# Attention feeding a two-layer network: products of a step before its ReLUs, wider rows for the first keys and values, other store rooms and queues

## The chip, the cores and the metric

The kernel runs on one core of a Trainium2 chip. The metric is the device time of one execution in microseconds. TensorE (PE) multiplies matrices into PSUM, VectorE (DVE) and ScalarE (ACT) work elementwise, GpSimd (POOL) helps, SyncE (SP) issues most transfers, and 16 DMA engines move the data.

## The reference

```python
# attention over 32 memories per head; batch 8, 8 heads, 576 tokens, 64 wide
a = exp(phi - max(phi, axis=2)); a = a / (sum(a, axis=2) + 1e-9)      # over tokens
k_m = einsum('bhsm,bhsd->bhmd', a, k); v_m = einsum('bhsm,bhsd->bhmd', a, v)
scores = q @ k_m.T / sqrt(64)
attn = softmax(scores)                                               # over the 32 memories
x = (attn @ v_m) as 4608 tokens x 512
h = maximum(x @ w_in, 0)                                             # 2048 wide
return (h * h) @ w_out                                               # 4608 x 512
```

## The kernel before, in words

The work has two stages, and its order on each engine is the order in which the program is written.

The **first layer** never builds x. For each batch, `exp_phi` takes the exponent of phi, `memories` multiplies it with keys and values into 32 memories per head (a column of ones beside the values, in rows of 130, sums the denominators), `make_u` multiplies the value memories with a quarter of w_in into `u`, and `attend` makes the attention weights `a` of one token tile. Both `u` and `a` are kept as a high and a low part. A batch has a wide tile (320 tokens) and a narrow one (256). One `step` makes 128 rows of h for both tiles: three products (high x high, low x high, high x low) for each of two groups of heads, so six products for a tile, into one half of the PSUM tile `h`, then a ReLU on ACT (L496) into a room `o`. PSUM has two such tiles (`ps_f`). Two steps fill a room `o`, and `spill` stores it to DRAM on SP's queue (L506); the room's name goes by the step's number within its batch, and there are two rooms.

There are 130 steps: 10 in an order written out by hand (`ORDER`, where S is a step and the letters are the next piece of a task), then 120 in the main loop, in which `plan` names for each task the half steps behind which its pieces are issued. The weights arrive as 64-bit words that `decode_in` and `decode_out` turn into floats. The loads of batch 1 are issued together by `loads_1`, those of later batches by `plan`: phi by `load_phi`, keys and values by `load_kv` (two transfers of 512-byte rows for each pair of row blocks), q by `load_q` into one of two rooms. `spin` issues products whose results nobody reads.

The **second layer** loads h back, squares it, and multiplies it with w_out by a scheme with seven products of half-size blocks in place of eight (`products`, L606). `rooms_m` holds its results before they are added and stored.

The pools `ffn` and `att` hold the rooms of the first layer; the pools `s` and `x` of the second layer take their place.

```python
            for j, (v, x, qd) in enumerate(todo):
                nc.tensor.matmul(
                    h[:, i, :T], u[:, v, qd, fs], a[x][:, qd], start=j == 0, stop=j == len(todo) - 1
                )
            nc.scalar.activation(r[:, f % 2, x0:x0 + T], h[:, i, :T], AF.Relu)
```

Of the kernel before, what the change touches and what calls it, by code (L numbers as in the profile page):

```python
# [1 line left out]

# [6 lines left out]
F32 = mybir.dt.float32  # L9
# [13 lines left out]
def attn_moe_kernel(ctx: ExitStack, tc: tile.TileContext, qT, kv, phi, w_in, w_out, outT):  # L23
# [4 lines left out]
    P = 128  # L28
# [40 lines left out]
    ident = const.tile([P, P], F32, name="ident")  # L69
    make_identity(nc, ident)  # L70
    warm = const.tile([P, 8], F32, name="warm")
    nc.gpsimd.memset(warm, 0.0)
    const.tile([P, 24], F32, name="gap_wo")
    wo = [None] * NP

# [8 lines left out]
    A_TILES = [(f"a_{n}{t}", t) for t in range(NT) for n in ("hi", "lo")]  # L84
    for n, t in A_TILES:
        ffn.tile([P, NQ * width(t)], F32, name=f"{n}_1")
    for i in range(2):
        ffn.tile([P, 2 * S], F32, name=f"o{i}")
    for n, t in A_TILES:
        keep.tile([P, NQ * width(t)], F32, name=f"{n}_0")  # L90
# [9 lines left out]
    e_sb = att.tile([P, FULL * NQ * P + P], F32, name="e_sb")  # L100
    e_full = e_sb[:, :FULL * NQ * P].rearrange("p (c x) -> p c x", c=FULL)
    e_rest = e_sb[:, FULL * NQ * P:]
    kv_full = [att.tile([P, FULL, 4, CW], F32, name=f"kv{qd}") for qd in range(NQ)]
    kv_rest = att.tile([P, 4, CW], F32, name="kv_rest")
    for t in kv_full:
        nc.gpsimd.memset(t[:, :, :, 2 * D:], 1.0)
    nc.gpsimd.memset(kv_rest[:, :, 2 * D:], 1.0)

    starting = [True]
    fine = [True]  # L110
# [67 lines left out]
    def load_kv(b, queues=None):  # L178

        queues = queues or 6 * [nc.sync]  # L180
        todo = [(qd, c) for c in range(0, FULL + 1, 2) for qd in range(NQ)]
        for (qd, c), queue in zip(todo, queues):
            if c < FULL:
                x = kv[b, qd, c * P:(c + 2) * P].rearrange("(c p) h x -> p c h x", p=P)
                for k in range(2):
                    queue.dma_start(out=kv_full[qd][:, c + k, :, :2 * D], in_=x[:, k])  # L186
            else:
                queue.dma_start(out=kv_rest[D * qd:D * (qd + 1), :, :2 * D], in_=kv[b, qd, FULL * P:])
            yield

    def memories(b):

        assert ("phi", b) in ready
        acc = pair()

        def add(qd, j, x, y, c):
            nc.tensor.matmul(  # L197
                acc[M * j:M * (j + 1), qd, :CW], x, y, start=(c == 0), stop=(c == FULL),
            )

        for c in range(FULL):
            for qd in range(NQ):
                for j in range(4):
                    at = qd * P + M * j
                    add(qd, j, e_full[:, c, at:at + M], kv_full[qd][:, c, j], c)
        for j in range(4):
            for qd in range(NQ):
                hs = slice(D * qd, D * (qd + 1))
                add(qd, j, e_rest[hs, M * j:M * (j + 1)], kv_rest[hs, j], FULL)
        if starting:  # L210
            spin(2)
        ready.add(("read", b))
        yield
        den = att.tile([P, NQ], F32, name="den")
        nc.vector.tensor_scalar_add(den, acc[:, :, 2 * D], EPS)
        nc.vector.reciprocal(den, den)
        kvn = att.tile([P, 2, NQ, 2, D], F32, name="kvn")
        for qd in range(NQ):
            x = acc[:, qd, :2 * D].rearrange("p (x d) -> p x d", x=2)[:, :, None, :].broadcast_to([P, 2, 2, D])
            if starting and qd == 0:  # L220
                nc.vector.tensor_scalar_mul(kvn[:, :, qd], x, den[:, qd:qd + 1])
            else:
                nc.scalar.activation(kvn[:, :, qd], x, AF.Copy, scale=den[:, qd:qd + 1])
        yield
        tp = pair()[:, 0]
        for i in range(2 * NQ):
            nc.tensor.transpose(
                tp[:, i * P:(i + 1) * P], kvn[:, i // NQ, i % NQ].rearrange("p a d -> p (a d)"), ident
            )
        if starting:  # L230
            spin(1, k=3)
        yield
        mem = mems[b] = keep.tile([P, 2, NPAIR, M], F32, name=f"mem{b % 2}")
        for half in range(2):
            copy = nc.vector.tensor_copy if starting and not half else nc.scalar.copy
            hs = slice(D * half, D * (half + 1))
            copy(mem[hs], tp[hs].rearrange("p (x r h m) -> p x r h m", x=2, r=NPAIR, h=2)[:, :, :, half])
        ready.add(("mem", b))
# [5 lines left out]

    def load_q(b, t):
        t0, t1 = tokens(t)
        x = q_at[b, t] = att.tile([P, NPAIR, t1 - t0], F32, name=f"q{t}")
        for i in range(2):
            nc.sync.dma_start(  # L249
                out=x[:, NQ * i:NQ * (i + 1)],  # L250
                in_=qT[b, NQ * i:NQ * (i + 1), :, t0:t1].rearrange("a p s -> p a s"),
            )
# [62 lines left out]
    def first_softmax(T, st, flat, at, mx, sm, sc):  # L315
# [10 lines left out]
        for i in range(NQ):  # L326
            nc.vector.tensor_reduce(out=mx[:, of[i]], in_=x[i], axis=AX.X, op=ALU.max)
            if i == 0:
                spin(3)
        for i in range(NQ):  # L330
            nc.vector.tensor_tensor(out=x[i], in0=x[i], in1=by_block(mx, i), op=ALU.subtract)
            nc.scalar.activation(x[i], x[i], AF.Exp, scale=SCALE)
        spin(1, mx[:, :1].broadcast_to([P, P]))
        yield
        for i in range(NQ):
            nc.vector.tensor_reduce(out=sm[:, of[i]], in_=x[i], axis=AX.X, op=ALU.add)
        nc.vector.tensor_scalar_add(sm, sm, EPS)
        nc.vector.reciprocal(sm, sm)
        spin(3, sm[:, :1].broadcast_to([P, P]))
        yield  # L340
        for i in range(NQ):
            nc.vector.tensor_tensor(out=x[i], in0=x[i], in1=by_block(sm, i), op=ALU.mult)
# [2 lines left out]
        yield  # L345
        a_hi, a_lo = new_a(0, 0)
        for i in range(NQ):
            spin(2, x[i][:, :P // M], k=2)
            nc.scalar.copy(a_hi[:, i], at[:, i])
        for i in range(NQ):  # L350
            nc.vector.tensor_tensor(out=a_lo[:, i], in0=at[:, i], in1=a_hi[:, i].bitcast(F32), op=ALU.subtract)
# [120 lines left out]
    steps += [(b, both, f) for b in range(2, B) for f in range(NFT)]  # L472
    BASE = {b: 2 * steps.index((b, both, 0)) for b in range(2, B)}
    open_pair = {}

    def step(b, ts, f):

        n = f * P // FC
        fs = slice(f * P % FC, f * P % FC + P)
        u = u_at[b, n][0]  # L480
        h = ps_f.tile([P, 2, 512], F32, name="f")
        assert ("u", b, f * P) in ready, (b, f)
        if f % 2 == 0:
            open_pair[ts] = ffn.tile([P, 2, sum(width(t) for t in ts)], F32, name=f"o{f // 2 % 2}")
        r = open_pair[ts]
        x0 = 0
        for i, t in enumerate(ts):
            assert ("a", b, t) in ready, (b, t, f)
            a = a_at[b, t]
            T = width(t)  # L490
            todo = [(v, x, qd) for qd in range(NQ) for v, x in ((0, 0), (1, 0), (0, 1))]
            for j, (v, x, qd) in enumerate(todo):
                nc.tensor.matmul(  # L493
                    h[:, i, :T], u[:, v, qd, fs], a[x][:, qd], start=j == 0, stop=j == len(todo) - 1
                )
            nc.scalar.activation(r[:, f % 2, x0:x0 + T], h[:, i, :T], AF.Relu)  # L496
            x0 += T
        u_at[b, n][2] -= len(ts)
        if not u_at[b, n][2]:
            u_free.append(u_at[b, n][1])  # L500

    def spill(b, ts, f):
        if f % 2:
            s0 = b * S + tokens(ts[0])[0]
            r = open_pair.pop(ts)
            nc.sync.dma_start(out=r_f32[f // 2][:, :, s0:s0 + r.shape[-1]], in_=r)  # L506


    def second_layer():
# [99 lines left out]
                    )  # L609

        def rooms_m():
            m = [sp.tile([P, 2, 2 * HALF], F32, name=n) for n in ("m01", "m23")]
            m.append(xp.tile([P, 2, 2 * HALF], F32, name="m45", bufs=1))
            m6 = xp.tile([P, 2 * HALF], F32, name="m6", bufs=1)
            xp.tile([P, 8], F32, name="gap_m", bufs=1)
            return [x[:, i] for x in m for i in range(2)] + [m6]
# [108 lines left out]
    def all_of(tasks):  # L725
        for _ in tasks:
            pass

    load_phi(0, nc.scalar)
    all_of(load_kv(0, (nc.scalar, nc.sync, nc.sync, nc.scalar, nc.scalar, nc.sync)))  # L730
    fetch_in(0, NQ)
    load_q(0, 0)
    load_q(0, 1)
    for n in (1, 2, 3):
        fetch_in(n)
    nc.scalar.activation(warm[:1, :1], warm[:1, :1], AF.Exp)
    spin(3)
    spin(1, k=2)

    def loads_1():  # L740
        load_phi(1)
        all_of(load_kv(1))
        load_q(1, 0)
        load_q(1, 1)
        for n in range(4, 8):
            fetch_in(n)

    first = {
        "e": lambda: exp_phi(0),
# [12 lines left out]
        "b1": lambda: attend(1, 1),  # L762
    }
    for n in range(8):
        first[f"d{n}"] = lambda n=n: decode_in(n, nc.gpsimd if n < 1 else None)

    ORDER = """
        e*6 m*4 L a d0 a d0*3 a d0 d1 a u0 a u0*2
        b S S b*4 d1*4 b*3 d2 b u1 b u1*2 S S S S
        d2*3 e1*2 d2 e1 u2 e1 u2*2 S S  # L770
        d3 e1*2 d3*3 e1 d3 m1*2 u3*3 S S m1*2
        d4 a1*4 d4*2 a1*3 d4*2 a1*2 d5 b1 a1 v0*3 b1*3 d5*2 b1*3 d5*2 b1*3 v1*3
    """
    tasks = {}
    ended = set()
    for x in ORDER.split():
        x, _, k = x.partition("*")
        for _ in range(int(k or 1)):
            if x == "S":
                s = run_step()  # L780
                spill(*s)
            elif x == "L":
                loads_1()
            else:
                if x not in tasks:
                    tasks[x] = first[x]()
# [10 lines left out]
    def pad(x):  # L797
        return [BASE[2] + h for h in x]

    plan = [  # L800
        ((20,), load_phi, 2),
        ((20, 20, 21, 21, 22, 22, 23), load_kv, 2),
        ((21, 23, 24), decode_in, 6),
        ((21,), load_q, 2, 0),
        ((22,), load_q, 2, 1),
        ((23, 25, 26), decode_in, 7),
        ((24, 25, 26), make_u, 0, 2),
        ((27, 28, 29, 30, 31, 32), exp_phi, 2),
# [3 lines left out]
        ((36, 38, 40, 42, 44, 46, 48), load_kv, 3),  # L812
        ((37, 38, 39), make_u, 0, 3),
        ((40, 41, 43, 44, 46, 48, 59), attend, 2, 0),
        ((42,), load_q, 3, 0),
        ((45, 46, 47), make_u, 1, 3),
        ((49, 50, 51, 52, 54, 60, 61), attend, 2, 1),
        ((53, 54, 55), make_u, 2, 0),
        ((60, 62, 63, 64, 65, 67), exp_phi, 3),
        ((61, 62, 63), make_u, 2, 1),  # L820
# [86 lines left out]
```

## Time and profile before

| | us |
|---|---|
| two runs | 894.57 and 905.2, median 899.88 |
| the profiled execution's own time | 902.26 |
| its span, first to last instruction | 900.4 |
| mean granted TensorE clock | 0.915 of full |
| busy: PE, DVE, ACT, POOL | 729.5, 558.6, 426.4, 21.5 |

Times in rows are microseconds from the start of the span. In a table of stretches each row has the stretch, its length, the busy time of each engine with its instructions, the granted TensorE clock as a share of full speed, the mean busy share of the DMA engines and GB/s. A row of the timeline has the start, the length, the engine, the line of the kernel, the operation, out<-in, and in brackets how long the engine stood idle before it and what ended that. A row of the chain has start, length and what ran. A row of waits has who waited for whom, total us, times, and the longest. PE's busy time contains the drain of its pipeline. The profile's L493 is the product of the first layer, L496 the ReLU, L606 the product of the second layer.

### The profile page before, as it was taken

The numbers are of one execution on the slowest core, as the hardware profiler recorded it, in microseconds if no ns is written. First come the engines' busy times: TensorE is split into PE (matmuls) and PEld (weight loads), VectorE is DVE, ScalarE is ACT, GpSimd is POOL, SyncE is SP. The second block draws the span as 40 slices with busy tenths as digits, with TensorE's granted clock in tenths as the row PEclk, the third lists the DMA queues.
The fourth block names the chain that finished last, engine by engine and source line by source line (L and its number), as shares of the span: only waits on it lengthen the run. The fifth ranks groups of instructions, "written<-read, shape, count | busy, mean of one in ns | idle before, by whom it ended". The sixth has DMA issues, their size and how long they took to land.

```text
span 900.4 us, 14642 instructions
## 1 busy us (share of the span) xinstructions
PE 729.5 (81%) x6122; PEld 627.8 (70%) x6122; DVE 558.6 (62%) x764; ACT 426.4 (47%) x582; POOL 21.5 (2%) x23
## 2 busy tenths in 40 slices
PE   7657557777686766777867768999999999999997
PEld 4345245555564654555645558999999999999997
DVE  2742671534634626537264244798988989898895
ACT  1413343344554434444434354466565565656652
POOL 0100000010100000001000000000000000000000
PEclk9955579999996989999989988899999999999999
DMA  9950714547648457474365727345435354453541
GB/s 276 306 211 27 210 47 133 193 152 243 240 140 273 160 185 259 154 227 162 130 239 199 246 102 289 113 128 153 145 113 164 109 155 145 132 160 110 153 134 54
DMA packets 107297, 152.47 MB, mean 169 GB/s; under 512 B 5600, under 2 KB 65504, under 8 KB 106208
## 3 DMA queue, kind: packets, MB, share of 16 engines
q1 hardware_dynamic: 104688, 150.30, 51.4%
q10 hardware_dynamic: 2544, 1.25, 0.6%
q8 instruction: 48, 0.79, 0.4%
q14 instruction: 17, 0.14, 0.0%
HBM read 95.94 MB, written 55.57 MB: 168 GB/s over the span
## 4 chain that ended last, share of the span: by engine, by line
PE 62%; ACT 12%; DMA 6%; DVE 5%; SPq 3%; issue 3%; POOL 0%; ACTq 0%; DVEq 0%; POOLq 0%
PE b L606 37%; PE f L493 19%; ACT o L496 5%; DMA r_f<-o 4%; PE u L260 3%; ACT u L367 2%; PE h L197 2%; DMA raw<-r_f 1%; SPq L186 1%; ACT low L386 1%; ACT tmp L385 1%; PE h L260 1%; DMA kv<-w_out_f 1%; ACT st L297 1%; SPq L249 0%
## 5 line engine op out<-in xcount | busy, mean ns | idle before, releaser
L493 PE MATMUL f<-a_hi,u 128*128 128x320 f32 (+1 forms) x1024 | 251.5, 338 | 131.2 <-ACT o L496 126.4
L493 PEld LDWEIGHTS f<-a_hi,u 128*128 128x128 f32 x1024 | 177.6, 210 | 202.2 <-ACT o L496 161.9
L496 ACT ACTIVATE o<-f 128x320 f32<-128x320 f32 (+1 forms) x256 | 105.0, 411 | 228.1 <-PE f L493 201.9
L543 ACT CAST x_hi<-y 128x1792 fp32r<-128x1792 f32 x72 | 122.1, 1696 | 134.6 <-PE b L606 60.8
L606 PE MATMUL b<-x_hi,s 128*128 128x256 f32 x1152 | 179.7, 279 | 0.0
L547 DVE TENSOR_TENSOR x_lo<-y,x_hi 128x1792 fp32r<-128x1792 f32 x72 | 145.5, 2021 | 37.7 <-ACT x_hi L543 37.7
L493 PE MATMUL f<-a_lo,u 128*128 128x320 f32 (+1 forms) x512 | 161.9, 316 | 0.0
L606 PEld LDWEIGHTS b<-x_hi,s 128*128 128x128 f32 x1152 | 154.4, 190 | 0.0
L606 PE MATMUL b<-x_hi,wo 128*128 128x256 f32 x864 | 134.1, 278 | 3.8 <-ACT x_hi L543 3.8
L537 DVE TENSOR_TENSOR y<-y 128x256 f32<-128x256 f32 (+1 forms) x216 | 110.6, 512 | 18.1 <-ACT y L525 13.1
L606 PEld LDWEIGHTS b<-x_hi,wo 128*128 128x128 f32 x864 | 115.0, 189 | 4.0 <-ACT x_hi L543 4.0
L606 PE MATMUL b<-x_lo,s 128*128 128x256 f32 x576 | 113.3, 278 | 0.0
L493 PEld LDWEIGHTS f<-a_lo,u 128*128 128x128 f32 x512 | 107.7, 210 | 0.2 <-DVE a_lo L312 0.2
L369 DVE TENSOR_TENSOR u<-u,u 128x1024 fp32r<-128x1024 f32 (+1 forms) x34 | 39.5, 1162 | 102.2 <-ACT u L367 102.0
L606 PEld LDWEIGHTS b<-x_lo,s 128*128 128x128 f32 x576 | 87.9, 190 | 0.0
L606 PE MATMUL b<-x_lo,wo 128*128 128x256 f32 x432 | 84.9, 278 | 1.3 <-DVE x_lo L547 1.3
L525 ACT ACTIVATE y<-raw 128x1024 f32<-128x1024 f32 x72 | 75.9, 1054 | 12.5 <-DMA raw<-r_f 12.5
L606 PEld LDWEIGHTS b<-x_lo,wo 128*128 128x128 f32 x432 | 65.7, 190 | 1.5 <-DVE x_lo L547 1.5
L260 PE MATMUL u<-w,mem 64*32 64x512 f32 (+1 forms) x544 | 42.9, 694 | 12.8 <-DVE u L369 8.4
L367 ACT CAST u<-u 128x1024 fp32r<-128x1024 f32 (+1 forms) x34 | 32.8, 963 | 19.7 <-PE u L260 19.7
L312 POOL TENSOR_TENSOR a_lo<-at,a_hi 128x640 fp32r<-128x640 f32 (+1 forms) x12 | 18.2, 1516 | 431.8 <-ACT a_hi L311 431.8
L626 DVE TENSOR_TENSOR m<-m,m 128x512 f32<-128x512 f32 x41 | 27.5, 686 | 0.7 <-ACT m L662 0.4
(91 smaller groups left out, 490.6 us busy)
## 6 DMA issues: line engine op xcount, KB each, us to landing
raw<-r_f SPq DMA_DIRECT2D x72, 512.0 KB, 4.1
r_f<-o SPq DMA_DIRECT2D x63, 576.0 KB, 3.6
kv<-in_kv SPq DMA_DIRECT2D x60, 256.0 KB, 6.3
out_t<-m SPq DMA_DIRECT2D x36, 256.0 KB, 2.2
wo<-in_w_out SPq DMA_DIRECT2D x8, 1024.0 KB, 6.3
wo<-in_w_in SPq DMA_DIRECT2D x7, 1024.0 KB, 10.7
q<-in_q SPq DMA_DIRECT2D x16, 320.0 KB, 5.7
e_sb<-in_phi SPq DMA_DIRECT2D x8, 512.0 KB, 4.3
```

Source lines behind the costliest of these rows:

```text
L260: nc.tensor.matmul(out[M * pr:M * (pr + 1), half, :y.shape[-1]], mem[hs, x, pr], y, start=True, stop=True)
L312: (nc.vector if fine else nc.gpsimd).tensor_tensor(out=a_lo, in0=at, in1=a_hi.bitcast(F32), op=ALU.subtract)
L367: nc.scalar.copy(u[:, 0, :, n0:n1], ps[:, :, :n1 - n0])
L369: nc.vector.tensor_tensor(out=u[:, 1, :, n0:n1], in0=ps[:, :, :n1 - n0], in1=u[:, 0, :, n0:n1].bitcast(F32), op=ALU.subtract)
L493: nc.tensor.matmul(h[:, i, :T], u[:, v, qd, fs], a[x][:, qd], start=j == 0, stop=j == len(todo) - 1)
L496: nc.scalar.activation(r[:, f % 2, x0:x0 + T], h[:, i, :T], AF.Relu)
L525: nc.scalar.activation(y[i][:, :4 * HALF], raw.pop(i).rearrange("p a n -> p (a n)"), AF.Square)
L537: nc.vector.tensor_tensor(out=out, in0=in0, in1=in1, op=ALU.subtract)
L543: nc.scalar.copy(x[i][0], y[i])
L547: nc.vector.tensor_tensor(out=x[i][1], in0=y.pop(i), in1=x[i][0].bitcast(F32), op=ALU.subtract)
L606: nc.tensor.matmul(acc[m][:, e * HALF:(e + 1) * HALF], w, x[i][u][:, z * HALF:(z + 1) * HALF], start=p == 0 and j == 0, stop=p == NP - 1 a ...
L626: nc.vector.tensor_tensor(out=out, in0=in0, in1=in1, op=ALU.add)
```

## The change

- `step` issues the products of both tiles, then the ReLUs of both.
- Rooms `o` are three and go round by a counter; the room `m45` of the second layer moves to the pool `s`.
- In the hand-written part, `spill` stores on ACT's queue.
- For batches 0 and 1 keys and values lie in rows of 128 (2 KB in DRAM and SBUF, one transfer for a pair of row blocks). The denominators come from products of the exponent with a tile `ones`.
- q has one room, and its loads are placed behind the scores that free it.
- The loads of the hand-written part are issued in pieces `L0` to `L5`; those of batch 2 move from `plan` into it.
- The first Exp on ACT moves ahead of the first loads; `decode_in(0)` adds on DVE; `spin` counts change.

```diff
-    nc.gpsimd.memset(warm, 0.0)
+    nc.gpsimd.memset(warm, 1.0)
+    ones = warm[:, :CW - 2 * D]
...
-    for i in range(2):
+    for i in range(3):
         ffn.tile([P, 2 * S], F32, name=f"o{i}")
...
+    def new_kv(cw):
+
+        kv_at["full"] = [att.tile([P, FULL, 4, cw], F32, name=f"kv{qd}") for qd in range(NQ)]
+        kv_at["rest"] = att.tile([P, 4, cw], F32, name="kv_rest")
+        if cw > 2 * D:
+            for t in kv_at["full"]:
+                nc.gpsimd.memset(t[:, :, :, 2 * D:], 1.0)
+            nc.gpsimd.memset(kv_at["rest"][:, :, 2 * D:], 1.0)
...
+        if b < 3:
+            new_kv(2 * D if b < 2 else CW)
...
-                for k in range(2):
-                    queue.dma_start(out=kv_full[qd][:, c + k, :, :2 * D], in_=x[:, k])
+                to = kv_at["full"][qd][:, c:c + 2]
+                if b < 2:
+                    queue.dma_start(out=to, in_=x)
+                else:
+                    for k in range(2):
+                        queue.dma_start(out=to[:, k, :, :2 * D], in_=x[:, k])
...
+        if cw < CW:
+            for c in range(FULL):
+                for qd in range(NQ):
+                    nc.tensor.matmul(
+                        acc[:, qd, 2 * D:CW], e_full[:, c, qd * P:(qd + 1) * P], ones, start=(c == 0), stop=False
+                    )
+            for qd in range(NQ):
+                hs = slice(D * qd, D * (qd + 1))
+                nc.tensor.matmul(acc[:, qd, 2 * D:CW], e_rest[hs], ones[hs], start=False, stop=True)
...
-        x = q_at[b, t] = att.tile([P, NPAIR, t1 - t0], F32, name=f"q{t}")
+        x = q_at[b, t] = att.tile([P, NPAIR, t1 - t0], F32, name="q")
...
-                spin(3)
+                spin(2)
...
         spin(1, mx[:, :1].broadcast_to([P, P]))
+        spin(1, x[0][:, :P // M])
+        spin(1, x[1][:, :P // M])
...
-        spin(3, sm[:, :1].broadcast_to([P, P]))
+        spin(1, sm[:, :1].broadcast_to([P, P]))
...
-            spin(2, x[i][:, :P // M], k=2)
+            spin(1, x[i][:, :P // M], k=2)
...
-            open_pair[ts] = ffn.tile([P, 2, sum(width(t) for t in ts)], F32, name=f"o{f // 2 % 2}")
+            open_pair[ts] = ffn.tile([P, 2, sum(width(t) for t in ts)], F32, name=f"o{next(o_turn) % 3}")
...
+        for i, t in enumerate(ts):
+            T = width(t)
             nc.scalar.activation(r[:, f % 2, x0:x0 + T], h[:, i, :T], AF.Relu)
...
-    def spill(b, ts, f):
+    def spill(b, ts, f, queue=nc.sync):
...
-            m = [sp.tile([P, 2, 2 * HALF], F32, name=n) for n in ("m01", "m23")]
-            m.append(xp.tile([P, 2, 2 * HALF], F32, name="m45", bufs=1))
+            m = [sp.tile([P, 2, 2 * HALF], F32, name=n) for n in ("m01", "m23", "m45")]
...
+    nc.scalar.activation(warm[:1, 4:5], warm[:1, 4:5], AF.Exp)
     load_phi(0, nc.scalar)
...
-    load_q(0, 1)
-    for n in (1, 2, 3):
-        fetch_in(n)
-    nc.scalar.activation(warm[:1, :1], warm[:1, :1], AF.Exp)
+    fetch_in(1)
...
+    loads = {
+        "L0": lambda: (load_q(0, 1), fetch_in(2)),
+        "L1": lambda: (load_b(1), fetch_in(3)),
+        "L2": lambda: (load_q(1, 0), fetch_in(4), fetch_in(5)),
+        "L3": lambda: (load_q(1, 1), fetch_in(6), fetch_in(7)),
+        "L4": lambda: (load_phi(2), all_of(load_kv(2))),
+        "L5": lambda: load_q(2, 0),
+    }
...
-        first[f"d{n}"] = lambda n=n: decode_in(n, nc.gpsimd if n < 1 else None)
+        first[f"d{n}"] = lambda n=n: decode_in(n)
...
-        e*6 m*4 L a d0 a d0*3 a d0 d1 a u0 a u0*2
-        b S S b*4 d1*4 b*3 d2 b u1 b u1*2 S S S S
+        e*6 m*4 L1 a L0 d0 a d0*4 a u0 d1 a u0 a u0
+        b L2 S S b*4 d1*4 b*3 d2 b u1 b u1*2 S S S S
...
-                spill(*s)
+                spill(*s, nc.scalar)
...
-        ((21,), load_q, 2, 0),
-        ((22,), load_q, 2, 1),
...
+        ((42,), load_q, 2, 1),
...
+        ((51,), load_q, 3, 0),
```

## Rows read from the trace of the kernel before

**Rows 1.** Stretches: hand-written steps, main loop, second layer.

```profile
38.00:110.00 72.00, 40.86 (x314) 28.62 (x298) 35.17 (x54) 22.69 (x37) 0.00 (x0) 0.59 0.51 169
110.00:542.00 432.00, 312.82 (x2628) 237.57 (x2621) 206.57 (x303) 192.88 (x363) 18.19 (x12) 0.91 0.54 182
542.00:900.40 358.40, 348.10 (x3025) 347.50 (x3024) 300.73 (x376) 200.78 (x168) 0.00 (x0) 0.98 0.46 142
```

**Rows 2.** Timeline of one plain step, PE and ACT.

```profile
497.20 0.50 PE L493 MATMUL f<-a_hi,u 128*128 128x256 f32 x2 [0.58 <-ACT o L496]
...
497.99 0.45 PE L493 MATMUL f<-a_hi,u 128*128 128x320 f32 x2
...
498.72 0.30 PE L493 MATMUL f<-a_lo,u 128*128 128x320 f32 x1
499.06 0.44 ACT L496 ACTIVATE o<-f 128x320 f32<-128x320 f32 x1 [0.49 <-PE f L493]
499.56 0.50 PE L493 MATMUL f<-a_hi,u 128*128 128x256 f32 x2 [0.53 <-ACT o L496]
```

**Rows 3.** Waits of PE from 110 to 542 us.

```profile
PE f L493 <- ACT o L496: 117.8, 120, 6.3
```

**Rows 4.** Stretches: the main loop's start, a batch's two halves, its end.

```profile
110.00:150.00 40.00, 26.42 (x234) 20.60 (x226) 22.54 (x32) 16.82 (x30) 0.00 (x0) 0.84 0.19 66
204.00:232.00 28.00, 18.68 (x218) 14.28 (x217) 11.93 (x17) 12.72 (x25) 1.53 (x1) 1.00 0.89 287
232.00:259.00 27.00, 20.52 (x162) 15.62 (x162) 17.63 (x25) 14.64 (x26) 1.45 (x1) 1.00 0.41 149
485.00:542.00 57.00, 40.25 (x242) 33.33 (x243) 21.02 (x34) 24.04 (x44) 0.00 (x0) 0.86 0.51 178
```

**Rows 5.** Chain that ended last, through the batch from 204 to 259 us.

```profile
204.01 2.29 PE h L197 x80
...
222.80 6.59 DMA r_f<-o
...
255.54 1.10 PE u L260 x16
...
259.14 2.30 PE h L197 x80
```

**Rows 6.** Timeline of early steps, PE and ACT.

```profile
50.74 0.41 PE L493 MATMUL f<-a_lo,u 128*128 128x256 f32 x1
...
56.01 0.66 ACT L496 ACTIVATE o<-f 128x256 f32<-128x256 f32 x2 [7.65 <-DMA r_f<-o]
...
56.45 0.90 PE L493 MATMUL f<-a_hi,u 128*128 128x320 f32 x2 [5.29 <-ACT o L496]
...
58.94 0.79 PE L493 MATMUL f<-a_hi,u 128*128 128x256 f32 x2 [0.53 <-ACT o L496]
```

**Rows 7.** Timeline of the start, ACT and PE.

```profile
0.73 1.23 ACTq L131 DMA_DIRECT2D e_sb<-in_phi  x2
...
10.85 1.28 ACT L736 ACT_TABLE_LOAD   x1 [10.85 <-DMA kv<-in_kv]
...
18.13 0.46 PE L197 MATMUL h<-kv_rest,e_sb 64*32 64x130 f32 x16 [0.99 <-DMA kv_rest<-in_kv]
```

**Rows 8.** Stretches: keys and values landing, then w_in and q.

```profile
5.00:13.00 8.00, 5.39 (x17) 2.54 (x15) 3.77 (x8) 2.14 (x3) 0.00 (x0) 1.00 1.13 282
19.00:28.00 9.00, 6.99 (x34) 2.76 (x32) 6.17 (x13) 5.71 (x8) 0.05 (x1) 1.00 1.02 383
```

**Rows 9.** Timeline of the first softmax, POOL and DVE.

```profile
27.95 2.38 POOL L403 TENSOR_TENSOR w<-tmp,low 128x1024 int32<-128x1024 int32 x1 [26.44 <-DVE tmp L396]
...
28.61 1.75 DVE L337 TENSOR_SCALAR sm<-sm 128x20 f32<-128x20 f32 x1
```

**Rows 10.** Timeline of the first exponent's products, PE.

```profile
8.04 0.71 PE L161 MATMUL h<-ident,nmx 128*128 128x128 f32 x4
```

**Rows 11.** One line's instructions (L249): all 32 loads of q.

```profile
DMA to landing us min/median/max: 3.3/5.9/7.7
```

More of the change, by code (lines that the diff above doesn't have):

```diff
@@ L1 @@
 from contextlib import ExitStack
+from itertools import count
 import concourse.bass as bass
@@ L102, in attn_moe_kernel @@
     e_rest = e_sb[:, FULL * NQ * P:]
[L103 to L107, printed above, removed]
+    kv_at = {}
+    def new_kv(cw):
[5 more added lines that the diff above has]
+            nc.gpsimd.memset(kv_at["rest"][:, :, 2 * D:], 1.0)
+    new_kv(CW)
     starting = [True]
@@ L184, in load_kv @@
                 x = kv[b, qd, c * P:(c + 2) * P].rearrange("(c p) h x -> p c h x", p=P)
-                for k in range(2):
-                    queue.dma_start(out=kv_full[qd][:, c + k, :, :2 * D], in_=x[:, k])
+                to = kv_at["full"][qd][:, c:c + 2]
[4 more added lines that the diff above has]
+                        queue.dma_start(out=to[:, k, :, :2 * D], in_=x[:, k])
             else:
-                queue.dma_start(out=kv_rest[D * qd:D * (qd + 1), :, :2 * D], in_=kv[b, qd, FULL * P:])
+                queue.dma_start(out=kv_at["rest"][D * qd:D * (qd + 1), :, :2 * D], in_=kv[b, qd, FULL * P:])
             yield
@@ L194, in memories @@
         acc = pair()
+        kv_full, kv_rest = kv_at["full"], kv_at["rest"]
+        cw = kv_rest.shape[-1]
         def add(qd, j, x, y, c):
             nc.tensor.matmul(
-                acc[M * j:M * (j + 1), qd, :CW], x, y, start=(c == 0), stop=(c == FULL),
+                acc[M * j:M * (j + 1), qd, :cw], x, y, start=(c == 0), stop=(c == FULL),
             )
+        if cw < CW:
[7 more added lines that the diff above has]
+                nc.tensor.matmul(acc[:, qd, 2 * D:CW], e_rest[hs], ones[hs], start=False, stop=True)
         for c in range(FULL):
@@ L474, in attn_moe_kernel @@
     open_pair = {}
+    o_turn = count()
     def step(b, ts, f):
@@ L505, in spill @@
             r = open_pair.pop(ts)
-            nc.sync.dma_start(out=r_f32[f // 2][:, :, s0:s0 + r.shape[-1]], in_=r)
+            queue.dma_start(out=r_f32[f // 2][:, :, s0:s0 + r.shape[-1]], in_=r)
     def second_layer():
@@ L732, in attn_moe_kernel, with load_b @@
     load_q(0, 0)
-    load_q(0, 1)
-    for n in (1, 2, 3):
-        fetch_in(n)
-    nc.scalar.activation(warm[:1, :1], warm[:1, :1], AF.Exp)
+    fetch_in(1)
     spin(3)
     spin(1, k=2)
[L740 to L746, printed above, removed]
+    def load_b(b):
+        load_phi(b)
+        all_of(load_kv(b))
+    loads = {
[6 more added lines that the diff above has]
+    }
     first = {
@@ L764, in attn_moe_kernel @@
     for n in range(8):
-        first[f"d{n}"] = lambda n=n: decode_in(n, nc.gpsimd if n < 1 else None)
+        first[f"d{n}"] = lambda n=n: decode_in(n)
     ORDER = """
-        e*6 m*4 L a d0 a d0*3 a d0 d1 a u0 a u0*2
-        b S S b*4 d1*4 b*3 d2 b u1 b u1*2 S S S S
+        e*6 m*4 L1 a L0 d0 a d0*4 a u0 d1 a u0 a u0
+        b L2 S S b*4 d1*4 b*3 d2 b u1 b u1*2 S S S S
         d2*3 e1*2 d2 e1 u2 e1 u2*2 S S
-        d3 e1*2 d3*3 e1 d3 m1*2 u3*3 S S m1*2
-        d4 a1*4 d4*2 a1*3 d4*2 a1*2 d5 b1 a1 v0*3 b1*3 d5*2 b1*3 d5*2 b1*3 v1*3
+        d3 e1*2 d3*3 e1 d3 m1*2 L4 u3*3 S S m1*2
+        d4 a1*2 L3 a1*2 d4*2 a1*3 d4*2 a1*2 d5 b1 a1 L5 v0*3 b1*3 d5*2 b1*3 d5*2 b1*3 v1*3
     """
@@ L780, in attn_moe_kernel @@
                 s = run_step()
-                spill(*s)
-            elif x == "L":
-                loads_1()
+                spill(*s, nc.scalar)
+            elif x in loads:
+                loads[x]()
             else:
@@ L800, in attn_moe_kernel @@
     plan = [
-        ((20,), load_phi, 2),
-        ((20, 20, 21, 21, 22, 22, 23), load_kv, 2),
         ((21, 23, 24), decode_in, 6),
-        ((21,), load_q, 2, 0),
-        ((22,), load_q, 2, 1),
         ((23, 25, 26), decode_in, 7),
@@ L814, in attn_moe_kernel @@
         ((40, 41, 43, 44, 46, 48, 59), attend, 2, 0),
-        ((42,), load_q, 3, 0),
+        ((42,), load_q, 2, 1),
         ((45, 46, 47), make_u, 1, 3),
         ((49, 50, 51, 52, 54, 60, 61), attend, 2, 1),
+        ((51,), load_q, 3, 0),
         ((53, 54, 55), make_u, 2, 0),
```

## The prediction

> **What bounds the kernel now.** I read the stretches first: which engine is nearly full, and at what clock [rows 1]. In the second layer (542 to 900.4 us) PE is busy for 348.1 of 358.4 us: that stretch is bounded by its products. In the first layer no engine is: from 110 to 542 PE shows 312.8 of 432 us, DVE 206.6, ACT 192.9, and the DMA share is 0.54. Where nothing is full, a chain of waits sets the time, so I looked at one plain step next [rows 2]. Its six products for the narrow token tile start at 497.20 and those of the next step's wide tile at 497.99. The wide tile's last product starts at 498.72, but the narrow tile's first one starts only at 499.56, 0.06 us after the ReLU of 499.06 (0.44 us long) has ended. So in each step PE stops between its two groups until ACT has read the first group, though the two groups write different halves of `h`. The waits add this up [rows 3]: 117.8 us in 120 waits, one for each of the 120 steps of this stretch. Everything else that PE waited for there is 1.2 us.
>
> The third view tells what will be next. One batch runs from one group of `memories` products to the next, 204.0 to 259.1 us, 55.1 us for 16 steps [rows 5]. Its two halves differ [rows 4]: 204 to 232 has a DMA share of 0.89 at 287 GB/s (the next batch's kv, q and phi, and the stores), 232 to 259 has 0.41 at 149 GB/s. I counted 7 steps in the first and 9 in the second, by the ReLUs of the wide tile. In the first half the chain runs through 6.59 us of a store's flight [rows 5].
>
> **The products before the ReLUs.** In steady work the wide group takes 497.99 to 498.72 plus one product of (498.72 - 497.99) / 5 = 0.15, which is 0.88 us; the narrow group, 0.79 us behind its wait, has about 0.1 us of exposed first weights in it, so 0.69. Twelve without a stop: 1.57 us, against a period of 499.56 - 497.20 = 2.36 us [rows 2]. The gap of 0.79 is a wait of 0.53 and 0.26 of drained pipeline, so the waits of 117.8 stand for 117.8 + 120 x 0.26 = 149 us at most; nothing below that excludes that much. What is late next: `ps_f` has two buffers, so a step's first product needs the ReLUs of two steps before. ACT needs 0.82 us a step for ReLUs, against 1.57 of PE, and falls behind only at its long tasks.
>
> I price the gain by the halves of a batch. Light half: 9 x 1.57 = 14.1, two groups of u products at 1.10 [rows 5] and about 1.5 for scores and exponent products (estimate, two groups like [rows 10]) make a floor of 17.8 us; ACT and DVE tasks in front of a ReLU give 2 us back (bounds 0 and 4, of the 27 - 17.8 = 9.2 that go); I take 20. Heavy half: PE needs 7 x 1.57 + 2.29 + 1.10 + 1.5 = 16, but the data is 28 us x 287 GB/s = 8.0 MB. At a share of 1 that rate is 287 / 0.89 = 322 GB/s, 25 us; at the best stretch of the trace, 383 GB/s [rows 8], 21 us. The third room for `o` lets PE run one more pair of steps ahead of the stores, so I take 23, with 21 and 28 (no gain) as ends. A batch is then 43 us, 12 less than now; six batches (150 to 485) save 72.
>
> The Trainium skill (DMA: Bandwidth & Descriptors, Specifications) puts the share of HBM for one core at about 358 GB/s; by that estimate the heavy half would take 22.4 us, 4 us less in six batches. The row of 383 GB/s lies above that figure, so the row stands.
>
> The two ends: 110 to 150 has DMA to spare (0.19) but a half-speed stretch and one wait of 6.3 us [rows 3, 4]; 8 steps x 0.79 = 6.3 and that wait give 13. From 485 to 542, 16 steps x 0.79 = 13, less 1 for the second layer's preparation, which has to be hidden under shorter steps: 12. Main loop: 72 + 13 + 12 = 97.
>
> **The stores: third room, ScalarE's queue.** Early on, PE stands from 51.15 to 56.45 because ACT waited 7.65 us for a store from the same room `o0` [rows 6]. The rooms now go round by threes, so that store is no longer waited for: 5.3 us. The six full steps before 110 lose their own waits, at half clock 0.53 and about 0.4 of drain each: 5.7. Issuing five stores on ACT costs it about 0.6 us each (as its two first ones, 1.23 us together [rows 7]); ACT is idle for two thirds of that stretch, so I cost them at nothing, 3 us if the cover is gone. The clock there is 0.59 of full [rows 1], near the lower level of 1.2 GHz; denser products may raise it, which I leave to the range (5 us).
>
> **The start.** The Exp table's load of 1.28 us stands just ahead of the first real Exp [rows 7]; moved to the front they delay ACT's three loads instead, the phi rest first: between -1.3 and +1.5. Keys and values in 2 KB rows: the stretch in which 512 B rows move has 282 GB/s, that with 4 KB and 1.2 KB rows 383 [rows 8]; 2.36 MB is 8.4 or 6.2 us, and the `memories` products end behind a wait for the last of it [rows 7]. So 0 to 2.2 us, and fewer issues on both queues. The new sums over `ones` are ten products per batch for two batches; by four products of 128 columns in 0.71 us [rows 10] they cost at most 1.8 us each time, hidden at batch 0 by the wait for kv, at batch 1 half in the way (+1). The decode's add goes from POOL to DVE: 2.38 us on POOL go, and with them the tiny DVE operation that took 1.75 beside it [rows 9]; DVE gets 1.23 us instead; zero. The spins are fillers. The split loads are issued piece by piece ahead of their users; q of the second tile now lies behind the loads of batch 1, so 0 with bounds of -1 and +2. Net: 2 us for the start and 10 for 38 to 110.
>
> The Trainium skill (DMA: Bandwidth & Descriptors, Specifications) speaks against the 2 KB rows: transfers from 512 B on already run at line rate, so they would bring nothing. The two rates above disagree with it here, though other traffic is mixed in; by the rule the forecast would be 2 us higher.
>
> **The second layer.** Its products and their order stay, and 348.1 of its 358.4 us are PE's [rows 1]; `m45` changes its room only. Nothing.
>
> **Sum.** The profiled execution took 902.3 us, 2.4 above the median of the two runs (899.9), a difference within their spread. 902.3 - 97 - 10 - 2 = 793.
>
> **The rivals.**
> 1. The data bounds more than I allow: the heavy half does not shrink at all, since stores lie behind loads in SP's one queue and ReLUs behind stores. For: 0.89 share, the store's flight of 6.59 on the chain. Against: the third room. Batch 48, 6 x 7 + 25 + 10 = 77 less: 825.
> 2. PE comes to bound the main loop: heavy half 21, light 18, ends 16 and 14, start and early part 17: 902 - 6 x 16 - 30 - 17 = 759.
> 3. It doesn't do what it says: PE waits for something else that ends with the ReLU, so the order changes nothing. Then only the early 5.3, the start and a few store waits go: 890. Against: the wait ends 0.06 us behind that very ReLU, step after step.
> 4. Slower: q has one room, so each q load can start only when the scores before it are taken, and SP holds the stores behind it. It decides from a landing later than 4 shortened steps, 9 to 10 us after the scores; at 20 us each of 13 attends stops PE for 10.3, +134: 927. Against: q loads land in 3.3 to 7.7 us [rows 11], and the plan already loaded behind the scores.
>
> **How the numbers follow.** Forecast 0.60, rival 1 0.20, rival 2 0.12, rival 3 0.04, rival 4 0.04. The range reaches from below rival 2 to past rival 1, which leaves out rivals 3 and 4 and tails of the others: 752 to 834. About 2% is what a measurement of this kernel can tell from no change (18 us). Faster than 882 are the forecast and rivals 1 and 2: 0.92; within it rival 3, 0.04; slower rival 4, 0.04.
>
> **What the profile after would show.** If the reading is right, the waits of PE for ReLUs in the main loop fall from 120 to under 50, groups of products come as twelve at about 1.57 us, batches last 41 to 46 us with a DMA share near 0.7, and ACT waits for stores or for DVE take the first places. The second layer stays at 358 us. Wrong would be: batches over 48 with stores on the chain (rival 1); the old stop of 0.53 in each step (rival 3); SP holding stores behind a q load (rival 4). The weakest term is the heavy half, where the third room and a faster DMA are taken together from one batch's share.

## The result and the profile after

The changed kernel takes 791.66 us (median of 2 runs, 791.18 to 792.15) against 899.88 before: a ratio of 0.880, 95% interval 0.857 to 0.902. Four further runs of it, beside seven of the kernel before on one chip, gave 794.37 against 905.08, 0.880 (0.875 to 0.886). The forecast was 793 in 752 to 834.

I cut both profiled executions at the same points: the starts of three ReLUs, counted from the first, and the end.

| stretch | before | after | change | forecast |
|---|---|---|---|---|
| start, to the 2nd ReLU | 40.35 | 38.92 | -1.4 | -2 |
| 2nd to 16th ReLU, the hand-written steps | 52.74 | 42.06 | -10.7 | -10 |
| 16th to 256th ReLU, the rest of the first layer | 449.16 | 350.86 | -98.3 | -97 |
| second layer | 358.15 | 358.46 | +0.3 | 0 |

The stretches of the changed kernel: the hand-written steps, the main loop, the second layer, then the two halves of one batch (columns: length, busy time and count of PE, PEld, DVE, ACT and POOL, granted clock, DMA share, GB/s).

```profile
37.00:99.00 62.00, 37.57 (x322) 28.80 (x323) 36.66 (x56) 22.89 (x38) 0.37 (x3) 0.71 0.56 185
99.00:432.00 333.00, 278.94 (x2621) 235.43 (x2620) 203.96 (x298) 179.26 (x363) 17.72 (x12) 0.93 0.70 237
432.00:790.30 358.30, 346.77 (x3020) 346.09 (x3020) 302.42 (x380) 200.73 (x168) 0.00 (x0) 0.99 0.46 142
173.90:192.70 18.80, 18.53 (x228) 15.75 (x228) 12.37 (x18) 11.73 (x25) 0.13 (x1) 1.00 0.84 259
192.70:216.90 24.20, 19.48 (x166) 16.07 (x170) 17.60 (x25) 14.13 (x28) 2.92 (x2) 0.93 0.80 297
```

Against [rows 1 and 4]: PE is busy for 0.84 of the main loop instead of 0.72, DVE and ACT do their old work in 100 us less, and the second layer is untouched. The half that lasted 28 us now takes 18.8 and is full of products (18.5 us busy); the other still has 4.7 us without any. One plain step on PE's timeline:

```profile
155.54 0.46 PE L523 MATMUL f<-a_hi,u 128*128 128x320 f32 x2
...
156.42 0.40 PE L523 MATMUL f<-a_hi,u 128*128 128x256 f32 x2
...
157.12 0.46 PE L523 MATMUL f<-a_hi,u 128*128 128x320 f32 x2
```

The next step's wide tile follows 1.58 us after this one's, with no idle time in brackets anywhere in between; it was 2.36 us with a stop [rows 2]. PE's waits in the main loop, 104 to 432 us (us in total, times, longest):

```profile
PE f L523 <- ACT o L528: 18.9, 12, 5.5
PE h L160 <- DVE phi_mx L155: 14.6, 6, 4.0
PE f L523 <- ACT a_hi L338: 5.0, 1, 5.0
PE h L287 <- DVE tmp L417: 3.9, 1, 3.9
PE h L254 <- ACT kvn L250: 3.6, 2, 2.0
PE h L287 <- DMA q<-in_q: 3.0, 2, 1.6
```

The 120 stops of [rows 3] have become 12 waits of 18.9 us, and the second place is new: products of the exponent that wait for DVE. ACT's own waits in the same stretch point to who is late behind those 12:

```profile
ACT o L528 <- PE f L523: 55.0, 39, 6.8
ACT a_hi L338 <- DVE at L335: 23.8, 11, 5.5
...
ACT kv L479 <- DVE kv L477: 13.8, 3, 7.7
...
ACT o L528 <- DMA r_f<-o: 3.5, 3, 2.3
```

ACT is held by PE, which is healthy, and then by DVE; stores hold it for 3.5 us only. The two longest of the 12, 5.5 and 4.5 us, follow ACT's waits of 7.7 and 3.1 us for DVE at L477, the sums of weights for the second layer.

### The profile page after: what moved, and what is told of

It reads as the page before. It is cut to its first block, busy times and chain, and to the rows that moved or that the text cites. A ratio compares the mean times of both kernels' runs of the same rounds, so it can differ in the third digit from the quotient of the medians.

```text
span 790.3 us, 14722 instructions
## 1 busy us (share of the span) xinstructions
PE 692.0 (88%) x6156; PEld 625.0 (79%) x6156; DVE 558.8 (71%) x765; ACT 412.8 (52%) x582; POOL 19.0 (2%) x25
## 4 chain that ended last, share of the span: by engine, by line
PE 63%; DVE 16%; DMA 9%; ACT 6%; issue 4%; SPq 1%; ACTq 0%; POOL 0%; DVEq 0%; POOLq 0%
PE b L638 42%; PE f L523 14%; DMA kv<-w_out_f 2%; PE h L215 2%; DMA q<-in_q 2%; DMA raw<-r_f 2%; PE u L287 1%; DVE u L398 1%; DVE tmp L425 1%; ACT o L528 1%; DMA r_f<-o 1%; DVE at L335 1%; DVE st L333 1%; PE h L287 1%; DVE sm L326 1%
## 5 line engine op out<-in xcount | busy, mean ns | idle before, releaser
L523 PE MATMUL f<-a_hi,u 128*128 128x320 f32 (+1 forms) x1024 | 230.4, 318 | 29.4 <-ACT o L528 18.9
L523 PE MATMUL f<-a_lo,u 128*128 128x320 f32 (+1 forms) x512 | 158.8, 310 | 0.0
L528 ACT ACTIVATE o<-f 128x320 f32<-128x320 f32 (+1 forms) x256 | 90.8, 410 | 106.4 <-PE f L523 70.3
L523 PEld LDWEIGHTS f<-a_lo,u 128*128 128x128 f32 x512 | 104.3, 204 | 0.4 <-DVE a_lo L339 0.4
L287 PE MATMUL u<-w,mem 64*32 64x512 f32 (+1 forms) x544 | 38.7, 620 | 8.3 <-DVE w L432 4.2
L287 PE MATMUL h<-q,mem 64*32 64x320 f32 (+1 forms) x256 | 15.9, 441 | 14.0 <-DMA q<-in_q 8.0
```

Of the source, the lines that this page charges most:

```text
L287: nc.tensor.matmul(out[M * pr:M * (pr + 1), half, :y.shape[-1]], mem[hs, x, pr], y, start=True, stop=True)
L523: nc.tensor.matmul(h[:, i, :T], u[:, v, qd, fs], a[x][:, qd], start=j == 0, stop=j == len(todo) - 1)
```

## The experiments

Each time is the median of 4 runs; a ratio is to seven runs of the kernel before on the same chip. Runs 1 to 4, 5 to 8 and 9 to 12 shared a chip each.

**1. The order of products and ReLUs alone**, in the kernel before.

```diff
+        for i, t in enumerate(ts):
+            T = width(t)
             nc.scalar.activation(r[:, f % 2, x0:x0 + T], h[:, i, :T], AF.Relu)
             x0 += T
```

> The kernel before with one edit: the products of both tiles of a step come before its ReLUs. Two store rooms, stores on SP's queue, all loads as before. My theory: the stop of 0.53 us in each of 120 steps goes, with the drain behind it; the two store rooms hold some back. 826 us, and PE's waits for ReLUs fall from 120 to under 60. Rival (stores and loads set the pace, the order only moves the wait): 860 us or more, with the waits of ACT for stores up from 13.7 us to over 40.

816.48 us (815.6 to 821.84), 0.907 (0.900 to 0.914): 88.6 us of the roughly 110 come from this edit. Its largest wait in the main loop (ACT's waits, 99 to 454 us) is now another one:

```profile
ACT o L498 <- DMA r_f<-o: 48.8, 14, 6.8
```

ReLUs wait for the stores that free their room: with short steps, two rooms are too few, as run 5 confirms.

**2. The old order, but a PSUM tile of its own for each token tile**, in the kernel before (the tile of `spin` is halved in the same way):

```diff
-        h = ps_f.tile([P, 2, 512], F32, name="f")
...
+            h = ps_f.tile([P, 512], F32, name=f"f{t}")
...
-                    h[:, i, :T], u[:, v, qd, fs], a[x][:, qd], start=j == 0, stop=j == len(todo) - 1
+                    h[:, :T], u[:, v, qd, fs], a[x][:, qd], start=j == 0, stop=j == len(todo) - 1
...
-            nc.scalar.activation(r[:, f % 2, x0:x0 + T], h[:, i, :T], AF.Relu)
+            nc.scalar.activation(r[:, f % 2, x0:x0 + T], h[:, :T], AF.Relu)
```

> The kernel before with its old order (six products, ReLU, six products, ReLU), but the two token tiles write two separate PSUM tiles instead of the two halves of one. Theory: PE stopped because the second group's first product was made to wait for the ReLU that reads the same PSUM tile, not because of the place of the ReLU in the program; so this gives the same as the step edit alone, within 8 us. Rival (the order itself matters): no gain, 890 to 900 us.

812.07 us (811.41 to 814.92), 0.901 (0.895 to 0.907). PE's waits from 99 to 454 us:

```profile
PE f L493 <- ACT o L496: 40.9, 19, 4.7
```

So the order was never the cause by itself. What stopped PE was that both halves belonged to one tile: the second group of products was made to wait for the reader of the first, though it writes elsewhere. The Trainium skill (PSUM — Partial Sum Buffer, PSUM bank collisions raise a hardware error) says that two engines may work in different banks at once; this run agrees, since a half of the tile is a bank and the 120 stops are gone without the new order.

**3. Everything but the order**: the changed kernel with each ReLU back behind its own products.

> The changed kernel with the old order inside a step; everything else of the change is in. Theory: only the early part (about 7 us up to the end of the hand-written steps) and the store waits of the main loop (some 10 us) are gained: 875 to 885 us, with 120 stops of 0.53 us left in the main loop. Rival (rooms and loads carry the gain): 840 us or less.

884.03 us (883.8 to 891.92), 0.982 (0.975 to 0.989). The old stop is whole, PE's waits from 104 to 525 us:

```profile
PE f L523 <- ACT o L526: 113.1, 120, 6.3
```

88.6 and 21.0 make 109.6 of the 110.7 us between the kernel before and the changed one here (run 4), but not because the parts are independent. From the 18th to the 256th ReLU the order alone saves 73.5 us (422.0 to 348.5), the rest alone 8 (413.9), both 97 (324.7): there they help each other. From the 2nd to the 16th they overlap: 9.5 and 7.1, together 10.7.

**4. The changed kernel once more**, beside the three above.

> The changed kernel once more, as the measure on this chip: 791 to 793 us.

794.37 us (791.64 to 796.09), 0.880 (0.875 to 0.886).

**5. Two store rooms** in the changed kernel.

```diff
-            open_pair[ts] = ffn.tile([P, 2, sum(width(t) for t in ts)], F32, name=f"o{next(o_turn) % 3}")
+            open_pair[ts] = ffn.tile([P, 2, sum(width(t) for t in ts)], F32, name=f"o{next(o_turn) % 2}")
```

> The changed kernel with its store rooms going round by twos (the third lies idle). In the step edit alone ACT waited 56.6 us for stores in 15 waits, in the whole change almost never. Theory: with steps shortened, the stores' flight is what the two rooms cannot cover; 806 us, with ACT's waits for stores over 40 us. Rival (the data rate bounds the main loop, a room more only moves the wait): within 3 us of the changed kernel, 791 to 797.

816.58 us (815.73 to 819.01), 0.905 (0.898 to 0.912): the time of run 1. So the third room is worth some 22 us, about all that the change gives beyond the order; I had it too low by ten. ACT's waits from 99 to 455 us:

```profile
ACT o L528 <- DMA r_f<-o: 47.0, 15, 6.1
```

and the chain that ended last, in a stretch with much data:

```profile
179.67 10.30 DMA r_f<-o
...
190.79 6.53 DMA r_f<-o
```

Two stores in a row, 10.3 and 6.5 us long, each freeing a room for the next pair of ReLUs.

**6. Rows of 130 for all batches**, so no sums over `ones` and no 2 KB rows.

```diff
-        if b < 3:
-            new_kv(2 * D if b < 2 else CW)
...
-                if b < 2:
+                if False:
                     queue.dma_start(out=to, in_=x)
                 else:
```

> The changed kernel with keys and values of all batches in rows of 130 with the ones column, as before: 512-byte rows, two transfers for a pair of row blocks, no products with ones. The trace of the changed kernel has these products on the path: 2.4 us at batch 0, 3.6 us at batch 1. Theory: they cost what the wider rows bring, so within 3 us of the changed kernel, 791 to 797. Rival 1 (512-byte rows are what held the start): 798 or more. Rival 2 (rows bring nothing, products cost all): 786 to 789.

787.66 us (786.68 to 794.89), 0.874 (0.867 to 0.882): no slower than the changed kernel, by the medians a few us faster. The sums show on PE's timeline of the changed kernel, at batch 0 and batch 1:

```profile
13.25 1.92 PE L222 MATMUL h<-warm,e_sb 128*128 128x2 f32 x16 [1.35 <-issue]
15.10 0.50 PE L227 MATMUL h<-warm,e_sb 64*128 64x2 f32 x4
15.53 3.45 PE L215 MATMUL h<-kv,e_sb 128*32 128x128 f32 x64
...
64.82 3.58 PE L222 MATMUL h<-warm,e_sb 128*128 128x2 f32 x16 [4.17 <-ACT e_sb L183]
...
68.85 1.51 PE L215 MATMUL h<-kv,e_sb 128*32 128x128 f32 x24
```

2.3 us (13.25 to 15.53) and 4.0 us (64.82 to 68.85), both times with PE waiting ahead of them, so they lie in the way. From the pair of ReLUs 11 and 12 to the pair 13 and 14 the changed kernel takes 17.9 us (60.24 to 78.09), this one 13.9 (59.86 to 73.78). In runs 4, 5, 7, 9 and 11, which keep the sums, that stretch takes 16.3 to 18.0, so between 2.4 us and all of the 4.0 at batch 1 come back. What the 2 KB rows give at batch 0 is less than the sums cost there: the last product of `memories` ends at 19.36 us in the changed kernel, at 18.21 here and at 18.59 before [rows 7].

**7. The loads of keys and values seven half steps later**, behind the load of q for the narrow tile.

```diff
-        ((4, 6, 8, 10, 12, 14, 16), load_kv, 2),
+        ((11, 13, 15, 17, 20, 22, 24), load_kv, 2),
```

(and so for each later batch)

> The changed kernel with the loads of keys and values of batches 3 to 7 seven half steps later in their batch, behind the load of q for the narrow tile. Theory: in the changed kernel the second half of a batch is held by that q load (9 us from the scores that free its room to its landing) and then by DVE's chain behind it; with the crowd of kv loads out of its way it lands earlier: 783 to 789 us. Rival (DVE bounds that half whatever q does): within 3 us of the changed kernel, 791 to 797. Second rival (the crowd now meets the stores): slower than 798.

792.41 us (789.62 to 792.84), 0.877 (0.871 to 0.884). No change that these runs resolve: the theory that these loads crowd q's, and with it hold the second half, falls.

**8. Two PSUM tiles and the old order** in the changed kernel (the edit of run 2).

> The changed kernel with the old order in a step, but two separate PSUM tiles for the two token tiles. Theory: no stop is left between the groups, as in the two-tile run on the old kernel, and the wide tile's PSUM is free earlier: 787 to 792 us, 2 to 5 below the changed kernel. Rival (the order matters once the other edits are in): 800 or more.

786.86 us (783.12 to 791.86), 0.874 (0.865 to 0.882). It does what the new order does; by the median it is 5 to 8 us faster, but its range touches those of the changed kernel.

**9. No loads of keys and values for batches 3 to 7**: these batches reuse what lies in SBUF, so their part of the output is not the reference's, and 11.8 MB less move.

```diff
         for (qd, c), queue in zip(todo, queues):
+            if b > 2:
+                yield
+                continue
```

> The changed kernel without the loads of keys and values of batches 3 to 7 (those of batch 2 stay in their rooms, so five batches are computed from the wrong keys and values): 11.8 MB less in the main loop. The prediction held that the first half of a batch is bounded by its 8 MB. If so, that half falls from 19 us towards PE's 16 and the light half shrinks too: below 775 us. Rival, the theory now (the rest of a batch's time is in DVE's chain, which PE waits for through the exponent's products): 783 to 790 us.

792.56 us (791.2 to 795.05), 0.880 (0.876 to 0.883). The stretches of this kernel: main loop, then the two halves of the same batch.

```profile
99.00:432.00 333.00, 278.87 (x2618) 237.35 (x2616) 202.38 (x298) 176.96 (x359) 17.76 (x12) 0.93 0.56 199
175.00:194.00 19.00, 18.88 (x230) 15.70 (x223) 11.76 (x18) 11.97 (x26) 0.91 (x1) 1.00 0.78 268
194.00:218.00 24.00, 18.90 (x134) 16.38 (x132) 16.97 (x25) 13.01 (x25) 2.16 (x2) 0.86 0.53 192
```

The DMA share falls from 0.70 to 0.56 and in the second half from 0.80 to 0.53, and no half gets shorter. The second half lost bytes, 7.2 MB to 4.6 (297 GB/s x 24.2 us and 192 x 24.0), so there the data does not set the time. The first half kept its own (259 x 18.8 and 268 x 19.0, 4.9 and 5.1 MB), so of that half this run says nothing.

**10. The low part of `w_out` on POOL**, eight operations off DVE.

```diff
-        nc.vector.tensor_tensor(out=wo[p][:, :, 1], in0=w, in1=wo[p][:, :, 0].bitcast(F32), op=ALU.subtract)
+        nc.gpsimd.tensor_tensor(out=wo[p][:, :, 1], in0=w, in1=wo[p][:, :, 0].bitcast(F32), op=ALU.subtract)
```

> The changed kernel with one operation of DVE moved to POOL: the low part of w_out, 8 times 1.22 us. Theory: DVE's chain is what the second half of a batch waits for now, so 4 to 8 us go: 784 to 789. Rival 1 (DVE has slack where this stands): 791 to 795. Rival 2 (POOL's operation slows DVE's neighbours, as one did in the first softmax of the kernel before): 796 or more.

799.88 us (795.03 to 804.4), 0.887 (0.882 to 0.892): slower than the changed kernel. The timeline of POOL and DVE tells why:

```profile
186.86 2.41 POOL L466 TENSOR_TENSOR wo<-tmp,wo 128x1024 fp32r<-128x1024 f32 x1 [23.66 <-ACT wo L463]
186.90 3.06 DVE L322 TENSOR_TENSOR st<-st,mx 128x640 f32<-128x640 f32 x1
...
207.12 2.67 POOL L466 TENSOR_TENSOR wo<-tmp,wo 128x1024 fp32r<-128x1024 f32 x1
207.63 2.45 DVE L153 TENSOR_TENSOR phi_mx<-st 128x256 f32<-128x256 f32 x1
```

DVE's subtraction of L322, 0.69 to 0.83 us in the changed kernel, takes 3.06 beside POOL's operation. Over the run its 15 instances take 16.3 instead of 11.3 us and the 8 of L153 9.8 instead of 7.8. So the run was no test of a lighter DVE: it made the two chains on DVE that PE waits for 7 us longer, and the time rose by about as much (7 to 10 us against runs 9 and 11).

**11. Early stores on SP's queue again.**

```diff
-                spill(*s, nc.scalar)
+                spill(*s)
```

> The changed kernel with the early stores on SP's queue, as before. Theory: five stores that nobody waits for with three rooms; within 3 us of the changed kernel, 789 to 797. Rival (SP's queue holds them behind loads until a room is missing): 798 or more.

790.08 us (789.31 to 791.46), 0.876 (0.873 to 0.880). The queue makes no difference that these runs resolve.

**12. Rows of 130 and two PSUM tiles together** (runs 6 and 8).

> The changed kernel with rows of 130 for all batches (no products with ones) and two separate PSUM tiles for the token tiles: the two edits that were faster alone. If their gains of some 5 us each are separate: 780 to 785 us. Rival (both shorten the same stretch): 786 to 789.

785.99 us (783.54 to 787.04), 0.872 (0.868 to 0.875), the fastest version. Its slowest run is 2 us below the fastest of run 11 on the same chip. The ratios' intervals just overlap, so this is some 4 us or 0.5% at the edge of what these runs resolve; the two savings do not add up in full.

## Why the prediction was right, and where it was not

**What bounded the kernel: right.** PE stopped once a step for the reader of a tile that it was about to write elsewhere; the stop is gone after, unchanged in run 3, and gone by another route in run 2. That excludes rival 3. The waits and drained pipeline of "149 us at most" gave back 98.3 in the main loop; plain steps run at 1.58 us where 1.57 was worked out.

**The heavy half: wrong, and this is the step of the sum that failed.** I held it to be bounded by its data at 23 us, from 8.0 MB at a share of 0.89: I took what moved within its 28 us for data that had to move within it. After the change 4.9 MB move in it (18.8 us x 259 GB/s), and the light half has 7.2 MB (24.2 x 297) where it had 4.0 (27 x 149) [rows 4]; a batch moves its 12 MB as before. The loads slid into the next half, and the only transfers that PE waited for in the main loop are those of q, for 3.0 us in all. The half takes 18.8 us in the batch shown. For means I cut five batches, from the 67th ReLU on, behind 14 and then 18 ReLUs each: the kernel before has 27.7 us, the order alone 24.5 (run 1), the changed kernel with two rooms 24.4 (run 5), with three 20.2. So the stop and the two rooms held that half: a ReLU waited until a store of one of two rooms had landed. I let the third room act only between ends of 21 and 25 us that bytes had set. Stores land later where more data moves (median 5.6 us in the changed kernel, 3.9 in run 9), so with two rooms bytes may still act through them; no run took data from a kernel with two rooms.

**The light half: too low.** Forecast 20, measured 24.2, on the mean of five 24.9. The floor of 17.8 counted PE's work; the 2 us that ACT and DVE tasks were to give back is 6 to 7, of which some 1.7 is PE's own (19.48 us busy, at a granted clock of 0.93). The chain that ended last runs through it in the changed kernel like this:

```profile
187.91 6.78 DMA q<-in_q
...
195.44 0.79 DVE st L317 x2
...
199.03 1.22 DVE tmp L425
...
202.98 1.11 DVE tmp L432
204.09 1.70 DVE st L149
...
206.71 0.71 PE h L160 x2
```

First a landing of q, which since the change has a single room and is issued behind the scores before it; then 11 us of DVE in one line: softmax (L317 to L335), the decoding of weights put between (L417 to L432), and the maximum for the next exponent, for which PE stands. That this half stays at 25 us with 11.8 MB less (run 9: 25.2), with keys and values moved (run 7) and with two store rooms (run 5: 25.0) excludes these three. The single room of q is not it either: with two, in runs 1 and 2, the half has 25.1 and 24.8 us, and in run 9 PE waits for no q in the main loop (here 3.0 us), while its wait for the products of the exponent rises to 20.3 us (here 14.6). Run 10, in which this DVE work grew and the time with it, speaks for DVE's chain; no run shortened that chain. So DVE is argued, not shown.

**The two errors cancel, by luck**: 18.8 and 24.2 make a batch of 43.0 us where 23 and 20 had made 43. On the mean of five a batch went from 58.4 to 45.2 us, 13.2 less instead of 12. The forecast's time was nearer than its reasons.

**Third room and early steps: right in sum, not in its parts.** 10.7 measured, 10 forecast as 5.3 + 5.7, less 1 for the sums. But the order alone gives 9.5 there although its ReLUs still wait 7.71 us for a store, and two rooms do not lengthen that stretch (run 5: 40.7 us against 42.1, and 40.4 in run 4): the two terms cover each other, and the sums over `ones` take some of what would be left (run 6: 36.7). The room's worth lies in the main loop, which I had not separated.

**The sums over `ones`: too small.** Priced at +1, by four products of 128 columns in 0.71 us [rows 10] and cover by a late kv [rows 7]. That row counts records, and a product in f32 leaves two of them (L161 issues two products, L222 eight): ten products by it are 20 records and 3.6 us, not 1.8. They cost 2.3 us at batch 0 and 4.0 at batch 1, where the granted clock was 0.50. The cover was gone: behind them no product of keys and values waits for a landing (15.53 and 68.85 us). As the Trainium skill has it (DMA: Bandwidth & Descriptors, Specifications), rows of 512 B lose nothing against wider ones; run 6 agrees as far as the whole time goes, by 787.66 us with 512 B rows against 791 to 794 with the sums and 2 KB rows. Whether wider rows land sooner no run resolves: with 512 B rows the products of `kv_rest` start, behind a wait for them, anywhere from 15.64 us (run 2) to 18.13 (before). My two rates [rows 8] were those of different traffic.

**Costed at nothing, and nothing:** the stores on ACT's queue (run 11), the second layer (+0.3). The start came out at -1.4 where -2 was forecast, but the 2nd ReLU of kernels that start alike lies anywhere from 37.5 (run 7) to 41.0 us (run 9), so neither figure is resolved.

**The rivals.** Rival 1 had the heavy half unmoved: refuted by the 18.8 us. Rival 4 had SP hold the stores behind q: PE waited 8.0 us for q in the whole run, three times, not once in each attend. Rival 2, PE as the bound, holds for the heavy half of the batch shown (18.5 of 18.8 us busy) and fails for the light one.

## What to carry to other kernels

In this kernel a wait between two groups of products that write different banks was a matter of how the tile is declared: give each reader its own tile, or issue all writers first. When such a stop goes, look at once for the buffer whose release was slow enough before: here one more store room was worth 22 us with the short steps, while with the long ones all of the change but the order gave 8 in the main loop (run 3). And before a stretch is called bounded by its data, ask which bytes have to move in it: of the heavy half's 8.0 MB some 3 moved into the next half, and in the whole main loop PE waited 3.0 us for transfers.

## What the runs showed of the hardware that was not expected

In these traces a DVE operation with two inputs in SBUF, beside one of POOL, stands until POOL is almost done. In run 10 L322 starts 0.04 us after POOL's 2.41 us and ends 0.69 us after it (189.96 against 189.27), where at this width it usually takes 0.83. A reduction, with its one input, keeps its length inside another of POOL's operations of that run, and the L322 behind it does not:

```profile
338.58 2.38 POOL L466 TENSOR_TENSOR wo<-tmp,wo 128x1024 fp32r<-128x1024 f32 x1 [3.60 <-ACT wo L463]
339.28 0.69 DVE L320 TENSOR_REDUCE mx<-st 128x16 f32<-128x512 f32 x1
340.00 1.51 DVE L322 TENSOR_TENSOR st<-st,mx 128x512 f32<-128x512 f32 x1
```

The changed kernel has one too, POOL's low part of `a` and the first maximum:

```profile
203.72 1.51 POOL L339 TENSOR_TENSOR a_lo<-at,a_hi 128x512 fp32r<-128x512 f32 x1 [9.60 <-ACT a_hi L338]
204.01 1.77 DVE L149 TENSOR_TENSOR st<-e_sb 128x512 f32<-128x512 f32 x1
```

L149 takes 0.69 us in its median instance; here it ends 0.55 us after POOL. The Trainium skill (SBUF — State Buffer, Who interferes with whom) has the rule: a DVE operation with two inputs in SBUF and a POOL operation that reads SBUF exclude each other. These pairs agree with it.

Products with only two columns are not cheap: 8 of them (16 records) with weights of 128 columns take 1.92 us at the start and 3.58 us at batch 1, while 24 records of 128 columns with weights of 32 take 1.51 right behind. The stretches of the two groups in the changed kernel tell the ratio: their granted clocks are 0.92 and 0.50, the lower level of 1.2 GHz.

```profile
64.80:68.90 4.10, 4.08 (x24) 4.05 (x28) 1.82 (x2) 0.00 (x0) 0.00 (x0) 0.50 0.00 0
13.20:15.60 2.40, 2.35 (x24) 2.35 (x28) 0.00 (x0) 0.00 (x0) 0.00 (x0) 0.92 1.09 283
```
